# A fused clustered attention and two expert layers: cosines summed in one bank, and where second-layer products stand in a stage's last unit

## The chip, the cores and the metric

One core of a Trainium2 chip runs the whole program. The metric is the device time of one execution in microseconds (us). Engines are named as in the profile: PE is TensorE, PEld its weight loads, DVE is VectorE, ACT is ScalarE, POOL is GpSimd, and SP issues most transfers.

## What is computed

Attention over 2 batches, 8 heads, 768 positions of 64 numbers, in which a query sees only the keys that fall into its own cluster (the nearest of 16 centroids by cosine); then a layer with a softplus, and then eight experts whose results are weighted by a Sinkhorn-balanced gate.

```python
q_assign = argmax(einsum('bhsd,hcd->bhsc', q_n, c_n), axis=-1)     # k_assign likewise
mask = q_assign[:, :, :, None] == k_assign[:, :, None, :]
scores = where(mask, q @ k.T / sqrt(D), -1e9);  attn = softmax(scores) @ v
x = attn.transpose(0, 2, 1, 3).reshape(1536, 512)
x = (softplus(x @ w_in)) @ w_out                                   # 512 -> 2048 -> 512
out = sum_e P[:, e:e+1] * (relu(x @ w1[e]) @ w2[e])                # 512 -> 1024 -> 512, e < 8
```

## The kernel before

Numbers that need full precision are split into a high and a low part (names ending in h and l, or hi and lo), and products are made of the parts.

**Attention** works on eight pairs of heads, g = 0 to 7. `sched_pair` gives every preparation step of a pair a place on a common scale, the attention steps of the pair before it have theirs, and all are issued in that order; a scheduler then places the instructions of each engine. For a pair, `pair_sims` multiplies queries and keys with the centroids: `Z` (and `Z0` for the first pair) holds each centroid's high part in one set of columns and its low part in another, so that one half of a pair (`hf`) takes four products `sm` of 384 columns, and 128 rows come out: high and low sums apart. ACT copies them to `sT`, PE turns them over (`tp`, three per half), ACT copies the low half to `s2`, and DVE adds the two into `A` (L457). `pair_argmax` and `pair_ohT` make one-hot rows of it, which are sent into the operand `Bt` of the scores. Meanwhile four half-heads a pair run: scores `s` (L561), their maximum on DVE (L569), the exponential on ACT (L574), transposes `t` of it (L601), their split into `eh` (ACT, L604) and `el` (DVE, L608), the products `av` (L616), and a copy `tmp` (ACT, L628) when a half's products are complete. `tp`, `sm`, `t` and others share three banks of PSUM.

**The layers** are four stages: the softplus layer for batch 0 and 1, eight units each, then the experts for batch 0 and 1, 32 units each. A unit multiplies x with one block of weights, in seven products `group` (i = 0 to 6; banks la, lb and mb) or, in the first stage, four products `plain_group` (L767), and then applies the activation (`act`, `act_split`: `gf`, then `gh` on ACT L803 and `gl` on DVE L804). A second layer of four parts (`layer2`, L823 and L842) belongs to each unit; it runs one unit later, its parts standing between the next unit's products. In the last unit of a stage (`final`) no part stands between them: four parts of the unit before and then the four of the last unit itself follow its products. During that unit `x_split` also makes the next stage's operands (`chA`, `clA`, `chS`, `clS`, L97 and L99).

Of the kernel before, what the change touches and what calls it, by code (L numbers as in the profile page):

```python
# [7 lines left out]
F32 = mybir.dt.float32  # L8
F32R = mybir.dt.float32r
# [3 lines left out]
ALU = mybir.AluOpType  # L13
# [7 lines left out]
def attention_moe_moe2(ctx, tc, q, k, v, qt, kt, centroids, w_in, w_out, w_gate, w1, w2, eye, out, dbg=None):  # L21
    nc = tc.nc
    B, H, S, D = q.shape
    NC_ = centroids.shape[1]
# [16 lines left out]
    idf = const.tile([P, P], F32, tag="idf", name="idf")  # L41
# [47 lines left out]
    def x_split(key, blk, i):  # L89
        name = FIRST[i] if key == "1_0" else COMBOS[i]  # L90
        shape, mq = [P, KC // 2, S // 2], slot_pool["mq"]
        hi = mq.tile(shape, F32R, tag=f"ch{i}", name=f"ch{name}{key}", bufs=1)
        lo = mq.tile(shape, F32R, tag=f"cl{i}", name=f"cl{name}{key}", bufs=1)
        if key == "1_0":
            copy_r(hi, blk[name])
        else:
            (nc.vector.tensor_copy if i == 0 else nc.scalar.copy)(hi, blk[name])  # L97
        eng = nc.gpsimd if key == "1_0" or i in (1, 4, 5) else nc.vector
        eng.tensor_tensor(lo, blk[name], hi.bitcast(F32), ALU.subtract)  # L99
        XC[name] = hi, lo  # L100
# [141 lines left out]
    pp = prep.enter_context(tc.tile_pool(name="pp", bufs=1, side="right"))  # L242
# [4 lines left out]
    ps_m = ps_t  # L247
# [37 lines left out]
    def prep_z(c2):  # L287
        for i in range(2):
            pc = ps_m.tile([P, P], F32R, tag="t", name=f"pc{i}")
            nc.tensor.transpose(pc, c2[:, i].rearrange("p a d -> p (a d)"), idr)  # L290
            pv = pc.bitcast(F32).rearrange("p (h j c) -> p h j c", j=2, c=NC_)
            nc.vector.tensor_copy(Z0[:, :, 96 + 16 * i : 112 + 16 * i], pv[:, 0])
            for j in range(2):
                js, o = slice(j * D, (j + 1) * D), 64 + 32 * j + 16 * i
                nc.vector.tensor_copy(Z[js, :, o : o + NC_], pv[js, :, j])

# [15 lines left out]
    def at(step, fn, cat=None):  # L314
        events.append((step, len(events), fn, cat))
# [112 lines left out]
    def pair_sims(st, hf, ph):  # L428
        g = st.g
        if ph == 0:  # L430
            if hf == 0:
                st.sT = pp.tile([P, 2, CB], F32, tag="sT", name=f"sT{g}", bufs=1)
                st.A = pp.tile([P, 2, HT * 4, NC_], F32, tag="A", name=f"A{g}", bufs=1)
            st.sm = ps_m.tile([P, CB], F32, tag="t", name=f"sm{g}{hf}")
            for n in range(4):
                w, x = divmod(n, 2)
                if g:
                    c, m = Z[:, st.hp, 64 - 64 * w : 192 - 64 * w], st.HL[w][:, x]
                else:
                    o = 64 * w + 32 * x  # L440
                    c, m = Z0[:, x, 96 - o : 224 - o], st.AT[w, x]
                nc.tensor.matmul(st.sm, c, m[:, hf * CB : (hf + 1) * CB], start=n == 0, stop=n == 3)
        else:
            nc.scalar.copy(st.sT[:, hf], st.sm)

    def pair_simsT(st, hf, ph):
        g = st.g
        if ph == 0:
            st.tp = ps_m.tile([P, HT * 4, 2, NC_], F32, tag="t", name=f"tp{g}{hf}")
            tpv = st.tp.rearrange("p (t x) a c -> p t (x a c)", t=HT)  # L450
            for t in range(HT):
                nc.tensor.transpose(tpv[:, t, :], st.sT[:, hf, t * P : (t + 1) * P], idf)
        elif ph == 1:
            st.s2 = pp.tile([P, HT * 4, NC_], F32, tag="s2", name=f"s2{g}{hf}", bufs=1)
            nc.scalar.copy(st.s2, st.tp[:, :, 1, :])
        else:
            nc.vector.tensor_tensor(st.A[:, hf], st.tp[:, :, 0, :], st.s2, ALU.add)  # L457
# [47 lines left out]
    def sched_pair(g, b0):  # L505
        def P_(step, cat, fn, *args):
            def f():
                fn(pairs[g], *args)

            prep_fns.add(f)  # L510
            at(step, f, (cat, g))

        b0 += (2.06, -2.82)[g] if g < 2 else 0.0
        at(b0 - 12.13, lambda: pair_load(g))
        for n in range(4) if g == 0 else ():
            P_(b0 - 7.54 + 1.5 * n, "sp", pair_split, n)
        for w in range(2) if g else ():
            for ph in range(2):
                P_(b0 - 7 + 0.5 * ph + 3 * w, f"sp{ph}", pair_split_t, w, ph)
            P_(g * SP - 31 + 2 * w, "sp2", pair_split_t, w, 2)  # L520
        for n in range(2):
            P_(b0 + n + 1.54, "sq", pair_norm, n)
            P_(b0 + 4.27 + 2 * n, "red", pair_norm, 2 + n)
        P_(b0 + 8.02, "ln", pair_norm, 4)
        P_(b0 + 8.36, "nw", pair_norm, 5)
        P_(b0 + (12.5 if g else 8.37), "nv", pair_norm, 6)
        for i in range(8) if g == 0 else ():
            d = 1.09 * i
            P_(b0 + d + 0.5, "t0", pair_trans, i, 0)
            P_(b0 + d + 0.72, "t1", pair_trans, i, 1)  # L530
            P_(b0 + d + 1.9, "t2", pair_trans, i, 2)
        for hf in range(2):
            P_(b0 + hf + 8.27, "sm", pair_sims, hf, 0)
            P_(b0 + hf + 8.27 + .1, "smc", pair_sims, hf, 1)
            P_(b0 + 2 * hf + 11.5, "tp", pair_simsT, hf, 0)
            P_(b0 + 2 * hf + 11.5 + .1, "tpc", pair_simsT, hf, 1)
            P_(b0 + 2 * hf + 11.5 + 0.65, "tpa", pair_simsT, hf, 2)
            P_(b0 + hf + 22.92, "oh", pair_ohT, hf, 0)
            P_(b0 + hf + 22.92 + .1, "ohc", pair_ohT, hf, 1)
        for ph, stp in enumerate((14.5, 17.14, 17.6, 19.78, 21.61)):  # L540
# [102 lines left out]
    for i in range(NHALF):  # L643
        g = i // 4
        for t in range(HT):
            n = 6 * i + 2 * t - LEAD
# [6 lines left out]
        for s in range(NT):  # L653
            n = 6 * i + s
# [7 lines left out]
        at(92 + (n - 1) * 1.36, lambda n=n: fetch_first(n), ("fu", 0))  # L662
    for n in range(4):
        at(175 + n * 5, lambda n=n: x_split("1_0", first_blk, n), ("xs", 0))
    KEEP = {'sp2': 1, 'fr': 0, 'sq': 1, 'red': 1, 'av': 1, 'am3': 1, 'tpa': 1, 'smc': 0, 'm0': 1, 'nw': 0, 'nv': 1, 'rw': 1, 'pz': 1, 'e1': 1, 'ln': 0}
    events.sort(key=lambda x: x[:2])
    last_prep = max(key for key, _, fn, _ in events if fn in prep_fns)
    open_mq = True
    for key, _, fn, cat in events:
# [206 lines left out]
    sm = mp.tile([P, 2], F32, tag="gm", name="gm", bufs=1)  # L876
# [60 lines left out]
    def run(*steps):  # L937
        for l in steps:
            for fn in l:
                fn()  # L940

    run(*split_unit(units[0]))
    pend = []
    starts = [n for n in range(len(units)) if n == 0 or units[n - 1][:2] != units[n][:2]]
    for n, u in enumerate(units):
# [4 lines left out]
        hold = 0 <= held < NHOLD  # L950
# [23 lines left out]
        for i in range(7):  # L974
            if not is_plain(u):
                group(u, i)
            elif i % 2 == 0:
                plain_group(u, i // 2)
            run(steps.get(i, []))
            if n + 1 in starts:  # L980
                key = f"{units[n + 1][0]}_{units[n + 1][1]}"
                if not is_plain(u):
                    x_split(key, sums, i)
                else:
                    for c in ((4,), (5,), (0, 1), (), (), (), (2, 3, 6))[i]:
# [66 lines left out]
```

## Time and profile before

| | us |
|---|---|
| runs of the program, median of 3 | 1617.62 (1617.32 to 1620.14) |
| the profiled execution | 1615.32 |
| its span, first to last instruction | 1613.5 |
| PE busy | 1536.4 |
| DVE busy | 1079.2 |
| ACT busy | 851.7 |

The profiled execution is 2.3 us shorter than the median of the runs. A busy share is a mean over attention (to about 290 us) and four stages, each with a limit of its own, so the stretches have to be read apart.

### The profile page before, as it was taken

The page shows a single profiled execution, that of the slowest core. Times are in us where ns is not written, and L with a number is a line of the kernel's source. Part 1 is how long each engine was busy: PE and PEld are TensorE (multiplying, and loading weights), DVE is VectorE, ACT ScalarE, POOL GpSimd, SP SyncE. Part 2 cuts the span into 40 slices and gives each one's busy share as a digit, 9 for nine tenths or more (in the row PEclk, how much of TensorE's full clock was granted, in tenths as well). Part 3 has the DMA queues.
Part 4 walks back from the last instruction along what each step waited for, and adds up shares of the span by engine and source line. Part 5 has one row for each costly group of instructions (what it writes and reads, how often), then busy time and mean ns, then how long its engine had stood idle before and what let it go on. Part 6 is the DMA issues. An engine that isn't in the chain of part 4 may idle for free.

```text
span 1613.5 us, 22747 instructions
## 1 busy us (share of the span) xinstructions
PE 1536.4 (95%) x8134; PEld 1381.5 (86%) x8134; DVE 1079.2 (67%) x1772; ACT 851.7 (53%) x1727; POOL 687.2 (43%) x681
## 2 busy tenths in 40 slices
PE   5899999888999989999999999999999999999999
PEld 4788888787897868899999999988999999999997
DVE  5999999998554768665655656577655556565553
ACT  5888988766676754343434434344434434344342
POOL 4444533334755743434434443345333343343430
PEclk8999999999999999999999999999999999999999
DMA  7666620364211221222323223223223232232211
GB/s 218 179 168 167 177 65 7 124 219 143 78 58 53 59 60 54 84 60 83 75 66 89 62 79 74 77 66 115 64 77 86 58 86 65 76 78 73 79 53 46
DMA packets 135971, 145.18 MB, mean 90 GB/s; under 512 B 9169, under 2 KB 100785, under 8 KB 135857
## 3 DMA queue, kind: packets, MB, share of 16 engines
q1 hardware_dynamic: 135712, 143.66, 31.4%
q8 instruction: 64, 1.05, 0.3%
q14 instruction: 51, 0.41, 0.1%
q10 hardware_dynamic: 144, 0.07, 0.0%
HBM read 113.23 MB, written 11.58 MB: 77 GB/s over the span
## 4 chain that ended last, share of the span: by engine, by line
PE 64%; DVE 7%; ACT 4%; issue 1%; POOL 1%; DMA 0%; DVEq 0%; ACTq 0%; POOLq 0%
PE Y L842 32%; PE la L714 16%; PE mb L714 8%; PE lb L714 4%; PE y L823 2%; DVE gf L790 1%; DVE gl L804 1%; DVE wl L226 1%; ACT gh L803 1%; ACT u L788 1%; ACT u L787 1%; PE p L767 1%; ACT u L789 1%; DVE xS L75 0%; ACT wh L225 0%
## 5 line engine op out<-in xcount | busy, mean ns | idle before, releaser
L803 ACT CAST gh<-gf 128x384 fp32r<-128x384 f32 x316 | 161.5, 513 | 479.2 <-DVE gf L797 434.5
L214 POOL TENSOR_TENSOR wf<-wf 128x256 f32<-128x256 f32 x288 | 237.3, 846 | 346.9 <-DMA wf<-in_moe_w_dram 273.7
L232 POOL TENSOR_TENSOR w2l<-w2f,w2h 128x512 fp32r<-128x512 f32 x160 | 240.3, 1522 | 314.4 <-ACT w2h L231 314.4
L842 PE MATMUL Y<-w2h,gh 128*128 128x512 f32 x768 | 299.0, 389 | 0.7 <-ACT gh L803 0.7
L842 PE MATMUL Y<-w2l,gh 128*128 128x512 f32 x768 | 298.8, 389 | 0.0
L842 PE MATMUL Y<-w2h,gl 128*128 128x512 f32 x768 | 298.5, 389 | 0.0
L804 DVE TENSOR_TENSOR gl<-gf,gh 128x384 fp32r<-128x384 f32 x316 | 207.2, 659 | 96.1 <-ACT gh L803 89.4
L741 DVE TENSOR_TENSOR gf<-la,c 128x384 f32<-128x384 f32 x71 | 39.5, 557 | 254.2 <-PE la L714 254.0
L225 ACT CAST wh<-wf 128x512 fp32r<-128x512 f32 (+1 forms) x232 | 153.0, 684 | 35.1 <-PE la L714 24.8
L842 PEld LDWEIGHTS Y<-w2h,gl 128*128 128x128 f32 x768 | 144.1, 188 | 30.1
L842 PEld LDWEIGHTS Y<-w2h,gh 128*128 128x128 f32 x768 | 144.0, 188 | 22.3 <-ACT gh L803 1.2
L842 PEld LDWEIGHTS Y<-w2l,gh 128*128 128x128 f32 x768 | 144.2, 188 | 21.0
L797 DVE SCALAR_TENSOR_TENSOR gf<-gf,pb 128x384 f32<-128x384 f32 x177 | 151.1, 854 | 4.0
L226 DVE TENSOR_TENSOR wl<-wf,wh 128x512 fp32r<-128x512 f32 (+1 forms) x194 | 151.9, 809 | 1.0 <-ACT wh L225 0.9
L608 DVE TENSOR_TENSOR el<-t,eh 128x384 fp32r<-128x384 f32 x192 | 101.5, 544 | 11.8 <-ACT eh L604 10.6
L601 PE MATMUL t<-idf,E 128*128 128x128 f32 x576 | 96.4, 276 | 8.3 <-DVE el L608 5.0
L714 PE MATMUL mb<-chS,wh 128*128 128x384 f32 x288 | 98.2, 341 | 4.3 <-DVE gf L737 4.0
L604 ACT CAST eh<-t 128x384 fp32r<-128x384 f32 x192 | 91.6, 481 | 19.3 <-PE t L601 11.6
L231 ACT CAST w2h<-w2f 128x512 fp32r<-128x512 f32 x160 | 92.3, 618 | 16.7 <-PE y L823 8.7
L714 PE MATMUL la<-chA,wh 128*128 128x384 f32 x288 | 97.8, 340 | 1.6 <-DVE gf L797 1.6
L569 DVE TENSOR_REDUCE sc<-s 128x1 f32<-128x768 f32 x96 | 91.1, 949 | 12.0 <-PE s L561 11.4
L733 ACT COPY c<-la 128x384 f32<-128x384 f32 x144 | 68.8, 478 | 57.2 <-PE la L714 55.9
(210 smaller groups left out, 3478.0 us busy)
## 6 DMA issues: line engine op xcount, KB each, us to landing
w2f<-in_moe_w_dram SPq DMA_DIRECT2D x128, 256.0 KB, 3.4
wf<-in_moe_w_dram SPq DMA_DIRECT2D x128, 256.0 KB, 3.4
AT<-HL SPq DMA_DIRECT2D x56, 192.0 KB, 4.0
r<-in_moe_w_in_dram SPq DMA_DIRECT2D x16, 512.0 KB, 5.8
r<-in_moe_w_out_dram SPq DMA_DIRECT2D x16, 512.0 KB, 5.2
pb<-pdram SPq DMA_DIRECT2D x15, 384.0 KB, 7.6
Bt<-HL SPq DMA_DIRECT2D x28, 192.0 KB, 4.1
w<-wf SPq DMA_DIRECT2D x16, 256.0 KB, 3.5
```

Of the source, the lines that this page charges most:

```text
L214: nc.gpsimd.tensor_tensor(wf[:, SLOT[o_], :], wf[:, SLOT[u_], :], wf[:, SLOT[v_], :], ALU.subtract)
L225: nc.scalar.copy(wh[:, c0:c1], wf[:, c0 + o : c1 + o, :])
L226: (nc.vector if kind == 2 or u == (1, 0, 0, 0) else nc.gpsimd).tensor_tensor(wl[:, c0:c1], wf[:, c0 + o : c1 + o, :], wh[:, c0:c1].bitcast ...
L231: nc.scalar.copy(w2h[:, c], w2f[c])
L232: nc.gpsimd.tensor_tensor(w2l[:, c], w2f[c], w2h[:, c].bitcast(F32), ALU.subtract)
L601: nc.tensor.transpose(pt[:, t * P : (t + 1) * P], Et[i, t][:, s * P : (s + 1) * P], idf)
L608: nc.vector.tensor_tensor(el, TT.pop((i, s)), EHL[i, s].bitcast(F32), ALU.subtract)
L714: nc.tensor.matmul(ps, wt[:, s_, ks], xx[:, k_, :], start=i in (0, 1, 3) and n == 0, stop=n == 3 * nk - 1, skip_group_check=True,)
L797: nc.vector.scalar_tensor_tensor(g, src, 0.0, PB[sb, e][:, cols], ALU.max, ALU.mult)
L803: nc.scalar.copy(gh[:, cols], g)
L804: nc.vector.tensor_tensor(gl[:, cols], g, gh[:, cols].bitcast(F32), ALU.subtract)
L842: nc.tensor.matmul(y[m], gt[:, ms], wt[:, q, :], start=first and i == 0, stop=last and i == 2)
```

## The change

The low parts of the centroids move into an operand of their own, and eight products per half instead of four add high and low parts into one bank of 64 rows. `tp` has 64 columns, ACT copies it straight to `A`, and `s2` and the addition on DVE are gone; the entry `tpa`, which had kept that addition behind what was issued before it, is gone too. In the last unit of a stage the first two parts of the second layer are issued after products 1 and 3 as in other units, and two parts are left for the end.

```diff
-    Z = pp.tile([P, NPAIR, 192], F32R, tag="Z", name="Z", bufs=1)
+    Z = pp.tile([P, NPAIR, 2, 96], F32R, tag="Z", name="Z", bufs=1)
...
-            st.sm = ps_m.tile([P, CB], F32, tag="t", name=f"sm{g}{hf}")
-            for n in range(4):
-                w, x = divmod(n, 2)
+            st.sm = ps_m.tile([64, CB], F32, tag="t", name=f"sm{g}{hf}")
+            for n in range(8):
+                w, x, i = n // 4, n // 2 % 2, n % 2
...
-                nc.tensor.transpose(tpv[:, t, :], st.sT[:, hf, t * P : (t + 1) * P], idf)
-        elif ph == 1:
-            st.s2 = pp.tile([P, HT * 4, NC_], F32, tag="s2", name=f"s2{g}{hf}", bufs=1)
-            nc.scalar.copy(st.s2, st.tp[:, :, 1, :])
-        else:
-            nc.vector.tensor_tensor(st.A[:, hf], st.tp[:, :, 0, :], st.s2, ALU.add)
+                nc.tensor.transpose(tpv[:, t, :], st.sT[:, hf, t * P : (t + 1) * P], idf[:64, :64])
+        else:
+            nc.scalar.copy(st.A[:, hf], st.tp)
...
-            P_(b0 + 2 * hf + 11.5 + 0.65, "tpa", pair_simsT, hf, 2)
...
-            if (i % 2 == 1 or i == 6) and pend and not hold and not final:
+            if (i % 2 == 1 or i == 6) and pend and not hold and (i < 4 or not final):
                 layer2(pend[0], i // 2)
...
             if final:
-                for part in range(4):
+                for part in range(2, 4):
                     layer2(p_, part)
```

Where instructions move, at three places.

ACT in the start-up, where the first pair's cosines are copied (`sT`, `s` or `A`) while the second pair's operands `HL` and squares of `rawq` and `rawk` are made. Before:

```order
L395 ACTIVATE s_165<-s_165 128x24
L444 COPY sT_226<-sm_228 128x384
L360 ACTIVATE HL_256<-rT_202 128x768
L444 COPY sT_226<-sm_240 128x384
L455 COPY s_254<-tp_250 128x192
L360 ACTIVATE HL_272<-rT_204 128x768
L455 COPY s_268<-tp_264 128x192
L383 ACTIVATE rawq_206<-rawq_206 128x768
L383 ACTIVATE rawk_208<-rawk_208 128x768
```

and in the changed kernel:

```order
L395 ACTIVATE s_165<-s_165 128x24
L360 ACTIVATE HL_263<-rT_202 128x768
L444 COPY sT_226<-sm_228 64x384
L360 ACTIVATE HL_276<-rT_204 128x768
L383 ACTIVATE rawq_206<-rawq_206 128x768
L444 COPY sT_226<-sm_244 64x384
L454 COPY A_227<-tp_258 128x192
L383 ACTIVATE rawk_208<-rawk_208 128x768
L454 COPY A_227<-tp_270 128x192
```

The second `sT` copy now stands behind both `HL` and the square of `rawq`, and the last copy, to `A`, behind `rawk` as well.

DVE in the last unit of the first stage (unit 7; `gf` and `gl` are its activation, `chA` and `clA` the next stage's operands). Before:

```order
L804 TENSOR_TENSOR gl_0_6_5277<-gf_0_6_5275,gh_0_6_5276 128x384
L97 CAST chA_1_5460<-x_70 128x768
L99 TENSOR_TENSOR clA_1_5461<-x_70,chA_1_5460 128x768
L790 SCALAR_TENSOR_TENSOR gf_0_7_5413<-p_0_7_5400,u_0_7_00_5416 128x384
L804 TENSOR_TENSOR gl_0_7_5415<-gf_0_7_5413,gh_0_7_5414 128x384
L790 SCALAR_TENSOR_TENSOR gf_0_7_5448<-p_0_7_5435,u_0_7_10_5451 128x384
L804 TENSOR_TENSOR gl_0_7_5450<-gf_0_7_5448,gh_0_7_5449 128x384
```

and in the changed kernel:

```order
L800 TENSOR_TENSOR gl_0_6_5309<-gf_0_6_5307,gh_0_6_5308 128x384
L786 SCALAR_TENSOR_TENSOR gf_0_7_5445<-p_0_7_5432,u_0_7_00_5448 128x384
L800 TENSOR_TENSOR gl_0_7_5447<-gf_0_7_5445,gh_0_7_5446 128x384
L97 CAST chA_1_5504<-x_70 128x768
L99 TENSOR_TENSOR clA_1_5505<-x_70,chA_1_5504 128x768
L786 SCALAR_TENSOR_TENSOR gf_0_7_5492<-p_0_7_5479,u_0_7_10_5495 128x384
L800 TENSOR_TENSOR gl_0_7_5494<-gf_0_7_5492,gh_0_7_5493 128x384
```

The first activation of unit 7, `gf` and `gl` (L786 and L800 are L790 and L804 of before), has moved ahead of `chA` and `clA`.

PE in the last unit of the third stage, from the end of its second product (bank lb) on; `Y` is the second layer. Before:

```order
L714 MATMUL lb_7_3_11285<-clA_0_6797,wh_7_3_11129 128x384
L714 MATMUL lb_7_3_11285<-chA_0_6796,wl_7_3_11131 128x384
L714 MATMUL la_7_3_11266<-chS_0_6810,wh_7_3_11129 128x384
L714 MATMUL la_7_3_11266<-clS_0_6811,wh_7_3_11129 128x384
L714 MATMUL la_7_3_11266<-chS_0_6810,wl_7_3_11131 128x384
L714 MATMUL la_7_3_11266<-chS_0_6810,wh_7_3_11129 128x384
L714 MATMUL la_7_3_11266<-clS_0_6811,wh_7_3_11129 128x384
L714 MATMUL la_7_3_11266<-chS_0_6810,wl_7_3_11131 128x384
L842 MATMUL Y_0_7623<-w2h_7_2_10989,gh_7_2_11144 128x512
L714 MATMUL mb_7_3_11318<-chS_0_6825,wh_7_3_11129 128x384
L714 MATMUL mb_7_3_11318<-clS_0_6826,wh_7_3_11129 128x384
```

and in the changed kernel:

```order
L710 MATMUL lb_7_3_11317<-clA_0_6829,wh_7_3_11161 128x384
L710 MATMUL lb_7_3_11317<-chA_0_6828,wl_7_3_11163 128x384
L838 MATMUL Y_0_7655<-w2h_7_2_11021,gh_7_2_11176 128x512
L838 MATMUL Y_0_7655<-w2l_7_2_11023,gh_7_2_11176 128x512
L838 MATMUL Y_0_7655<-w2h_7_2_11021,gl_7_2_11177 128x512
L838 MATMUL Y_1_7656<-w2h_7_2_11021,gh_7_2_11176 128x512
L838 MATMUL Y_1_7656<-w2l_7_2_11023,gh_7_2_11176 128x512
L838 MATMUL Y_1_7656<-w2h_7_2_11021,gl_7_2_11177 128x512
L838 MATMUL Y_2_7657<-w2h_7_2_11021,gh_7_2_11176 128x512
L838 MATMUL Y_2_7657<-w2l_7_2_11023,gh_7_2_11176 128x512
L838 MATMUL Y_2_7657<-w2h_7_2_11021,gl_7_2_11177 128x512
L710 MATMUL la_7_3_11298<-chS_0_6854,wh_7_3_11161 128x384
```

Nine products of the second layer, one part, now stand behind lb, and none behind the third product; the next part stands behind mb.

## Rows read from the trace of the kernel before

**Rows 1.** The page: span, and busy time of each engine.

```profile
span 1613.5 us, 22747 instructions
...
PE 1536.4 (95%) x8134; PEld 1381.5 (86%) x8134; DVE 1079.2 (67%) x1772; ACT 851.7 (53%) x1727; POOL 687.2 (43%) x681
```

**Rows 2.** Windows: us, then PE, PEld, DVE, ACT, POOL busy (instructions), PEclk, DMA, GB/s.

```profile
160.28:191.82 31.54, 29.68 (x196) 26.95 (x195) 29.56 (x60) 28.49 (x65) 15.59 (x21) 1.00 0.64 181
254.00:285.00 31.00, 28.99 (x192) 26.33 (x191) 28.24 (x53) 26.02 (x59) 5.28 (x6) 1.00 0.00 1
```

**Rows 3.** Timeline of TensorE: start, us, line, what.

```profile
162.36 0.87 PE L442 MATMUL sm<-HL,Z 128*128 128x384 f32 x4
163.06 0.49 PE L601 MATMUL t<-idf,E 128*128 128x128 f32 x3
163.31 0.60 PE L561 MATMUL s<-AT,AT 128*128 128x384 f32 x2
```

**Rows 4.** Timeline of ScalarE, the copy that closes each half's product.

```profile
162.83 0.48 ACT L628 COPY tmp<-av 64x384 f32<-64x384 f32 x1
...
171.02 0.47 ACT L628 COPY tmp<-av 64x384 f32<-64x384 f32 x1
...
178.27 0.48 ACT L628 COPY tmp<-av 64x384 f32<-64x384 f32 x1
...
187.07 0.47 ACT L628 COPY tmp<-av 64x384 f32<-64x384 f32 x1
...
263.80 0.47 ACT L628 COPY tmp<-av 64x384 f32<-64x384 f32 x1
...
270.85 0.48 ACT L628 COPY tmp<-av 64x384 f32<-64x384 f32 x1
```

**Rows 5.** Timeline of VectorE, last of one arg-max's four steps.

```profile
178.16 0.55 DVE L480 TENSOR_TENSOR OH<-A,mx 128x384 fp32r<-128x384 f32 x1
```

**Rows 6.** Groups by line, 0 to 300 us: busy, mean ns, idle before.

```profile
L457 DVE TENSOR_TENSOR A<-tp,s 128x192 f32<-128x192 f32 x16 | 5.6, 348 | 1.9 <-ACT s L455 1.9
...
L455 ACT COPY s<-tp 128x192 f32<-128x192 f32 x16 | 5.2, 327 | 0.8 <-ACT E L574 0.4 <-PE tp L452 0.2
```

**Rows 7.** Timeline of all engines, start-up.

```profile
12.14 2.30 PE L442 MATMUL sm<-AT,Z 128*128 128x384 f32 x8
...
14.89 0.47 ACT L444 COPY sT<-sm 128x384 f32<-128x384 f32 x1
...
16.40 0.87 ACT L383 ACTIVATE rawq<-rawq 128x768 f32<-128x768 f32 x1
...
16.95 1.27 DVE L469 TENSOR_TENSOR A<-A,nrm 128x384 f32<-128x384 f32 x1
...
24.55 2.85 PE L442 MATMUL sm<-HL,Z 128*128 128x384 f32 x8
...
25.34 2.47 SPq L501 DMA_DIRECT2D Bt<-OHT  x4
...
28.29 0.95 PE L561 MATMUL s<-Bt,Bt 80*128 80x384 f32 x4 [0.89 <-DMA Bt<-OHT]
```

**Rows 8.** Windows of TensorE: us, PE busy (instructions), PEclk, DMA, GB/s.

```profile
31.00:37.00 6.00, 6.00 (x22) 0.50 0.97 236
```

**Rows 9.** Timeline of TensorE, last units of three stages: idle time before it.

```profile
426.68 0.44 PE L767 MATMUL p<-chA,wh 128*128 128x384 f32 x1 [1.83 <-DVE gf L790]
...
565.40 0.44 PE L714 MATMUL mb<-chS,wh 128*128 128x384 f32 x1 [1.59 <-DVE gf L737]
...
584.15 0.62 PE L823 MATMUL y<-gl,w2h 128*128 128x512 f32 x2 [1.99 <-DVE gl L804]
...
1089.58 0.45 PE L714 MATMUL mb<-chS,wh 128*128 128x384 f32 x1 [1.77 <-DVE gf L737]
```

**Rows 10.** Timeline of VectorE at the end of the third stage.

```profile
1098.59 3.71 DVE L804 TENSOR_TENSOR gl<-gf,gh 128x384 fp32r<-128x384 f32 x3
```

**Rows 11.** The chain that ended last, end of the program.

```profile
1593.37 16.33 PE Y L842 x72
```

More of the change, by code (lines that the diff above doesn't have):

```diff
@@ L251, in attention_moe_moe2 @@
         nc.gpsimd.memset(wsel[:, :, c : c + 1], float(NC_ - c))
-    Z = pp.tile([P, NPAIR, 192], F32R, tag="Z", name="Z", bufs=1)
-    Z0 = pp.tile([P, 2, 224], F32R, tag="Z0", name="Z0", bufs=1)
+    Z = pp.tile([P, NPAIR, 2, 96], F32R, tag="Z", name="Z", bufs=1)
+    Z0 = pp.tile([P, 2, 2, 112], F32R, tag="Z0", name="Z0", bufs=1)
     def norm_newton(o, x, s0, eng):
@@ L291, in prep_z @@
             pv = pc.bitcast(F32).rearrange("p (h j c) -> p h j c", j=2, c=NC_)
-            nc.vector.tensor_copy(Z0[:, :, 96 + 16 * i : 112 + 16 * i], pv[:, 0])
+            nc.vector.tensor_copy(Z0[:, :, i, 48:64], pv[:, 0])
             for j in range(2):
-                js, o = slice(j * D, (j + 1) * D), 64 + 32 * j + 16 * i
-                nc.vector.tensor_copy(Z[js, :, o : o + NC_], pv[js, :, j])
+                js, o = slice(j * D, (j + 1) * D), 32 + NC_ * j
+                nc.vector.tensor_copy(Z[js, :, i, o : o + NC_], pv[js, :, j])
     def last_of_engines(engines):
@@ L431, in pair_sims @@
             if hf == 0:
-                st.sT = pp.tile([P, 2, CB], F32, tag="sT", name=f"sT{g}", bufs=1)
+                st.sT = pp.tile([64, 2, CB], F32, tag="sT", name=f"sT{g}", bufs=1)
                 st.A = pp.tile([P, 2, HT * 4, NC_], F32, tag="A", name=f"A{g}", bufs=1)
-            st.sm = ps_m.tile([P, CB], F32, tag="t", name=f"sm{g}{hf}")
-            for n in range(4):
-                w, x = divmod(n, 2)
+            st.sm = ps_m.tile([64, CB], F32, tag="t", name=f"sm{g}{hf}")
+            for n in range(8):
+                w, x, i = n // 4, n // 2 % 2, n % 2
                 if g:
-                    c, m = Z[:, st.hp, 64 - 64 * w : 192 - 64 * w], st.HL[w][:, x]
+                    c, m = Z[:, st.hp, i, 32 - 32 * w : 96 - 32 * w], st.HL[w][:, x]
                 else:
-                    o = 64 * w + 32 * x
-                    c, m = Z0[:, x, 96 - o : 224 - o], st.AT[w, x]
-                nc.tensor.matmul(st.sm, c, m[:, hf * CB : (hf + 1) * CB], start=n == 0, stop=n == 3)
+                    o = 32 * w + 16 * x
+                    c, m = Z0[:, x, i, 48 - o : 112 - o], st.AT[w, x]
+                nc.tensor.matmul(st.sm, c, m[:, hf * CB : (hf + 1) * CB], start=n == 0, stop=n == 7)
         else:
@@ L448, in pair_simsT @@
         if ph == 0:
[L449 to L450 removed]
+            st.tp = ps_m.tile([P, HT * 4, NC_], F32, tag="t", name=f"tp{g}{hf}")
+            tpv = st.tp.rearrange("p (t x) c -> p t (x c)", t=HT)
             for t in range(HT):
[L452 to L455 removed]
+                nc.tensor.transpose(tpv[:, t, :], st.sT[:, hf, t * P : (t + 1) * P], idf[:64, :64])
         else:
[L457 removed]
+            nc.scalar.copy(st.A[:, hf], st.tp)
     def pair_argmax(st, ph):
@@ L664, in attention_moe_moe2 @@
         at(175 + n * 5, lambda n=n: x_split("1_0", first_blk, n), ("xs", 0))
-    KEEP = {'sp2': 1, 'fr': 0, 'sq': 1, 'red': 1, 'av': 1, 'am3': 1, 'tpa': 1, 'smc': 0, 'm0': 1, 'nw': 0, 'nv': 1, 'rw': 1, 'pz': 1, 'e1': 1, 'ln': 0}
+    KEEP = {'sp2': 1, 'fr': 0, 'sq': 1, 'red': 1, 'av': 1, 'am3': 1, 'smc': 0, 'm0': 1, 'nw': 0, 'nv': 1, 'rw': 1, 'pz': 1, 'e1': 1, 'ln': 0}
     events.sort(key=lambda x: x[:2])
```

## The prediction, made before the changed kernel ran

> **What bounds the kernel now.** I read the page first: PE is busy 1536.4 of 1613.5 us [rows 1], so on the whole TensorE sets the time. That mean hides where it waits. The timeline of PE with its idle times shows no wait at all in the last stage, and only a few in the others; those in the last units of the first three stages are [rows 9]. Attention, to about 290 us, is the other place that the change touches, and there the page cannot say who sets the pace: over one pair (31.5 us) PE is busy for 29.7 us and DVE for 29.6 us [rows 2].
>
> The copies that close each half-head settle it [rows 4]. Without any preparation beside it a half takes 270.85 - 263.80 = 7.05 us. The half from 171.02 to 178.27 holds a whole arg-max on DVE, four steps of about 0.55 us each [rows 5], and takes 7.25 us: 2.2 us more for DVE cost 0.2 us. The half from 162.83 to 171.02 has little more for DVE, but a group of `sm` and both groups of `tp` on PE, and takes 8.19 us. The half behind 178.27, in which PE turns over the one-hot rows and waits for them, takes 8.80 us. So more PE work makes a half longer, and more DVE work hardly does. In attention PE sets the pace, with about 1.9 us of idle time in a pair [rows 2].
>
> **The added products.** Four `sm` run from 162.36 to 163.06 [rows 3]: 0.175 us each. The change has eight more for a pair: 1.40 us. Six of the eight pairs are prepared beside running halves, which makes 8.4 us of PE work. That is the upper bound; the lower is what is left if the 1.9 us of idle time per pair took in most of it. I don't see PE idle near the `sm` in the timeline, but a part of its waits for `el` later in the pair should shrink, because DVE loses two additions of 0.348 us [rows 6] and each half lasts longer. The six transposes of a pair also have 64 columns instead of 128; three of the present shape take 163.31 - 163.06 = 0.25 us [rows 3], so half of two such groups, 0.25 us a pair, is the most that can go, and I take half of that. I take 1.40 - 0.13 - 0.4 = 0.85 us a pair, **+5.0 us for six pairs**, with +1.5 (0.25 us a pair) and +8.4 (nothing given back) as bounds.
>
> A product with a stationary operand half as wide fills half of the array, and one could hope that it costs half. The trace of before has no `sm` of 64 columns. The Trainium skill (TensorE: Matmul & The Clock Gate, "Wait — 56ns, not 53.3ns?") speaks against that hope and so against this change: the distance from one product to the next is the number of moving columns over the clock plus about 2.5 ns, with nothing of the stationary width in it. By that rule 384 columns are an estimated 162 ns and the six pairs cost 7.8 us where my rows give 8.4 us.
>
> **The removed additions.** Sixteen on DVE, 0.348 us each, 5.6 us [rows 6], of which twelve lie in the running part (4.2 us). Since a half hardly notices DVE work, I book nothing beyond the 0.4 us a pair above. If DVE were the limit after all, they would give 4.2 us. The copy on ACT stays; it only writes `A` in place of `s2`.
>
> **The start-up** is a chain: cosines of pair 0, copies, arg-max, one-hot rows, the transfer to `Bt`, first complete score. Two things make it later. First the copies. Now eight `sm` run from 12.14 to 14.44 and the arg-max begins at 16.95 [rows 7]. After the change the first `sT` copy can start when eight are done, about 14.5. Behind it stand, by the order, `HL`, `rawq`, the second `sT`, a copy to `A`, `rawk` and the last copy: 0.47 + 0.87 + 0.87 + 0.47 + 0.33 + 0.87 + 0.33 = 4.2 us with the durations of [rows 6, 7] (`HL` and `rawk` taken as long as `rawq`). The arg-max then begins at 18.7: +1.8 us. Second, the `sm` of pair 1 stand on PE ahead of the first scores with `Bt`. Eight take 2.85 us there, and the scores now begin at 28.29, 0.89 us after them, when the transfer is in. Shifted by 1.8 us, sixteen begin at 26.35 and end between 30.5 (second half at the full clock) and 31.9 (all at the pace of 2.85 us for eight), while the transfer is in at 30.1. So the first scores start 2.2 to 3.6 us later; I take 2.6.
>
> Some of this can come back. From 31 to 37 us PE is busy without a break at a granted clock of 0.50, the 1.2 GHz level [rows 8]; before that, between 27.4 and 31 us, it had done little but the four scores at 28.29 [rows 7]. With twice the products PE is busier ahead of this stretch, and at the full clock its six us would be three. The Trainium skill (TensorE: Matmul & The Clock Gate, "Part 1: The HAM clock gate") says that the array starts at half its clock and that sustained activity releases it, which would make this gain likely; the trace agrees in that the low clock follows the idle stretches. I book a third of the 3 us: the start-up is **+1.6 us**, from -0.8 (2.2 - 3.0) to +3.6.
>
> **The last units of stages.** The second layer's instructions stay the same in number, so only waits can go.
>
> - First stage: product 3 waits 1.83 us for `gf`, which has to empty its bank and stands behind `chA` and `clA` on DVE [rows 9]. Now `gf` stands ahead of them, and two parts of some 2.1 us each lie between. The whole wait goes: -1.8 us. The end stays covered: two parts of the unit before, 4.2 us, and the first of the unit's own stand ahead of the one that needs the last product.
> - Second stage: the wait of 1.59 us at 565.40 is covered by a part. But the end of this stage waits for DVE: the last `gl` is awaited at 584.15 for 1.99 us [rows 9]. DVE and ACT have the same work as before ahead of that `gl`, with fewer products to cover it. I take -1.2 us; 0 and -2.0 are the bounds.
> - Third stage: the wait of 1.77 us at 1089.58 [rows 9] is covered in the same way. The three last `gl` ran from 1098.59 to 1102.3 [rows 10], just in time for the last unit's own parts, which followed without a wait; those would now come some 2 us earlier and wait for them. I take -1.2 us, from 0 to -2.0.
> - Fourth stage: the trace has no wait; the second layer runs as one block of 16.33 us, 72 products, to the end [rows 11]. Where 18 of them stand changes nothing: 0.
>
> Sum **-4.2 us**, from -1.8 to -5.8.
>
> **Sum**: +5.0 + 1.6 - 4.2 = +2.4 us. Against the profiled execution's own 1615.3 us that is 1617.7. The runs' median lies 2.3 us above that execution, so I forecast 1620.0 us. A measurement of this kernel can tell about 0.2% (3.2 us) from no change, and +2.4 is within that.
>
> **Rivals.**
>
> - *Slower: every added product is paid.* Place: PE's queue in the halves that prepare a pair. For it speaks that no idle time stands near the `sm`, against it that 1.9 us a pair stand elsewhere. Price 8.4 instead of 5.0: 1.6 + 8.4 - 4.2 = +5.8, 1623.4 us. It decides once a pair lasts over 32.9 us where [rows 2] have 31.5. Chance 0.20.
> - *Slower: the waits at the stage ends only move.* DVE in the second and third stage is late in any case, and the change doesn't do there what it says; only the first stage gains. 5.0 + 1.6 - 1.8 = +4.8, 1622.4 us. For it: the waits on `gl`; against: in the third stage there is none now. Chance 0.16.
> - *Faster: DVE sets the pace of attention.* For it: PE's waits there are mostly for `el`, and DVE is as busy as PE. Against: the half with the arg-max. Then -4.2 for the additions, the products hide in PE's idle time, and 1.6 - 4.2 - 4.2 = -6.8, 1610.8 us. Chance 0.18.
> - *The clock stays up in the start-up*: -0.8 in place of +1.6, sum 0, 1617.6 us. Chance 0.14.
>
> **How the numbers follow.** My forecast keeps 0.32; its own range, from half its terms' bounds, is 1616 to 1624 us. Of it 0.20 fall within 0.2%, 0.08 above and 0.04 below. The first rival is slower (0.20), the second mostly (0.10 of 0.16), the third faster (0.18), the fourth the same, with 0.04 faster. That makes faster 0.26, same 0.36, slower 0.38. The terms' bounds together reach from -5.1 (all low) to +10.2 us; leaving out half of the faster rival and the sum of all high bounds gives 1612 to 1626 us.
>
> **What the changed profile would show.** Halves with `sm` longer by about 0.5 us, a pair at 32.4 us, and DVE's busy share in attention lower. The first score with `Bt` at 30.5 to 31 us instead of 28.29. No wait of PE for `gf` in the last units of the first three stages, but 1 to 2 us of waiting for `gl` behind them in the second and third. I am wrong if a pair gets shorter, if the clock in the start-up changes much, or if the scheduler's other order in attention, which moves many scores and transposes by a place or two, costs or gives more than the counted work.

## The result, and the profile after

The changed kernel takes 1630.83 us (median of 4 runs, 1629.65 to 1632.31), the kernel before 1618.82 us beside it. The ratio is 1.0079, with a 95% interval of 1.0067 to 1.0091: 12 to 13 us slower, above the range of 1612 to 1626 us. In what follows, us on the kernel before are ratio minus 1, times 1618.

The page of the changed kernel, span and engines; its counterpart is [rows 1]:

```profile
span 1630.5 us, 22858 instructions
...
PE 1555.6 (95%) x8198; PEld 1389.1 (85%) x8198; DVE 1081.1 (66%) x1756; ACT 853.6 (52%) x1727; POOL 687.3 (42%) x681
```

PE has 64 products more, and 19 us more of busy time. The windows over one pair, from the first `sm` of one to the first `sm` of the next, with columns as in [rows 2]:

```profile
168.72:202.95 34.23, 31.68 (x204) 27.46 (x202) 29.00 (x56) 28.85 (x65) 15.25 (x21) 1.00 0.51 134
```

A pair took 31.54 us and takes 34.23. PE is busy 2.0 us longer, DVE 0.6 us less, and PE's idle time did not shrink: 1.86 us before, 2.55 now. The timeline of PE in that pair says what the products cost:

```profile
168.72 1.54 PE L442 MATMUL sm<-HL,Z 128*64 128x384 f32 x8
170.09 0.51 PE L557 MATMUL s<-AT,AT 128*128 128x384 f32 x2
...
177.61 0.40 PE L452 MATMUL tp<-idf,sT 64*128 64x64 f32 x3
177.94 0.61 PE L557 MATMUL s<-AT,AT 128*128 128x384 f32 x2
```

Eight products with a stationary operand of 64 columns last 1.37 us up to the next instruction, 0.171 us each; the four of 128 columns took 0.70 us [rows 3]. So the width of that operand gives nothing back. The Trainium skill (TensorE: Matmul & The Clock Gate, "Wait — 56ns, not 53.3ns?") has only the moving columns in its rule, and the trace agrees: 0.171 us with 64 stationary columns, 0.175 with 128. The three narrow transposes `tp` take 0.33 us up to what follows, three wide ones in the same pair of the kernel before 0.32:

```profile
165.13 0.49 PE L452 MATMUL tp<-idf,sT 128*128 128x128 f32 x3
165.45 0.49 PE L601 MATMUL t<-idf,E 128*128 128x128 f32 x3
```

The copies that close a half on ACT:

```profile
189.39 0.48 ACT L624 COPY tmp<-av 64x384 f32<-64x384 f32 x1
...
198.19 0.47 ACT L624 COPY tmp<-av 64x384 f32<-64x384 f32 x1
...
206.06 0.48 ACT L624 COPY tmp<-av 64x384 f32<-64x384 f32 x1
...
215.52 0.47 ACT L624 COPY tmp<-av 64x384 f32<-64x384 f32 x1
...
223.65 0.48 ACT L624 COPY tmp<-av 64x384 f32<-64x384 f32 x1
```

The half with the one-hot rows still takes 8.80 us, as in [rows 4]; the one with the second group of `sm` and `tp` takes 9.46 us, where a like half took 8.19.

At one place in attention PE waits longer than the kernel before does anywhere behind its first score with `Bt` (there 1.71 us at most). It is where PE turns over the one-hot rows `OH` of the third pair, whose last step runs on POOL. The timeline of PE at this place, before and then after:

```profile
82.00 0.50 PE L490 MATMUL po<-idr,OH 128*64 128x128 f32 x3 [1.07 <-DVE el L608]
```

```profile
85.72 0.38 PE L487 MATMUL po<-idr,OH 128*64 128x128 f32 x3 [2.36 <-POOL OH L480]
```

The place lies in the second four halves. Cut at the copies `tmp`, these four are, before and then after:

```profile
81.42:113.69 32.27, 29.96 (x188) 26.83 (x189) 30.02 (x61) 28.67 (x64) 16.64 (x20) 0.95 0.62 158
83.84:119.73 35.89, 31.98 (x200) 28.72 (x201) 33.09 (x63) 29.59 (x66) 17.39 (x22) 0.95 0.63 166
```

PE's idle time in them grew from 2.31 to 3.91 us. The mean granted clock (PEclk) is 0.95 in both: it falls here in either kernel, so the fall is no part of the difference.

Start-up, all engines (counterparts in [rows 7]):

```profile
12.06 4.55 PE L442 MATMUL sm<-AT,Z 128*64 128x384 f32 x16
...
16.74 0.46 ACT L444 COPY sT<-sm 64x384 f32<-64x384 f32 x1
...
18.05 0.30 ACT L454 COPY A<-tp 128x192 f32<-128x192 f32 x1
...
18.39 1.23 DVE L466 TENSOR_TENSOR A<-A,nrm 128x384 f32<-128x384 f32 x1 [3.46 <-ACT A L454]
...
24.52 5.08 PE L442 MATMUL sm<-HL,Z 128*64 128x384 f32 x16
...
29.43 0.87 PE L557 MATMUL s<-Bt,Bt 80*128 80x384 f32 x4
```

The arg-max begins 1.4 us later, behind the last copy to `A`, which waits its turn on ACT. The first score with `Bt` follows right behind the sixteen products of the second pair, which run to 29.6 us, and is only 1.1 us later than before. Last, the end of the third stage on PE (counterpart: 1089.58 in [rows 9]) and on DVE (counterpart: [rows 10]):

```profile
1104.11 0.45 PE L710 MATMUL mb<-chS,wh 128*128 128x384 f32 x1 [0.84 <-DVE gf L733]
...
1110.37 0.44 PE L710 MATMUL la<-chA,wh 128*128 128x384 f32 x1 [0.75 <-DVE gf L737]
...
1118.27 0.50 PE L838 MATMUL Y<-w2h,gl 128*128 128x512 f32 x1 [2.01 <-DVE gl L800]
```

```profile
1114.04 2.62 DVE L99 TENSOR_TENSOR clA<-x,chA 128x768 fp32r<-128x768 f32 x1
1116.58 3.19 DVE L800 TENSOR_TENSOR gl<-gf,gh 128x384 fp32r<-128x384 f32 x2
```

One wait of 1.77 us has become three, of 3.6 us together. The last stage still ends with one block of the second layer, now of 54 products instead of 72 [rows 11], 17.0 us later:

```profile
1614.47 12.25 PE Y L838 x54
```

Between the two profiled executions, attention (up to the first `p` of the layers: 289.73 and 305.33) accounts for 15.6 of these 17.0 us. The profiled execution of before is 3.5 us under the median of its runs, that of after 1.5 us above, so 5.0 us of the 17.0 come from the choice of executions.

### The profile page after: what moved, and what is told of

It is laid out like the page before. It is cut to its first block, busy times and chain, and to the rows that moved or that the text cites. A ratio compares the mean times of both kernels' runs of the same rounds, so it can differ in the third digit from the quotient of the medians.

```text
span 1630.5 us, 22858 instructions
## 1 busy us (share of the span) xinstructions
PE 1555.6 (95%) x8198; PEld 1389.1 (85%) x8198; DVE 1081.1 (66%) x1756; ACT 853.6 (52%) x1727; POOL 687.3 (42%) x681
## 4 chain that ended last, share of the span: by engine, by line
PE 63%; DVE 8%; ACT 4%; issue 1%; DMA 1%; POOL 0%; DVEq 0%; ACTq 0%; SPq 0%; POOLq 0%
PE Y L838 31%; PE la L710 16%; PE mb L710 8%; PE lb L710 4%; PE y L819 3%; DVE gf L786 1%; DVE gl L800 1%; PE p L763 1%; DVE wl L226 1%; ACT gh L799 1%; ACT u L784 1%; DVE gf L793 1%; ACT u L783 1%; DVE xS L75 1%; ACT u L785 1%
## 5 line engine op out<-in xcount | busy, mean ns | idle before, releaser
L800 DVE TENSOR_TENSOR gl<-gf,gh 128x384 fp32r<-128x384 f32 x316 | 207.4, 659 | 96.3 <-ACT gh L799 89.7
L793 DVE SCALAR_TENSOR_TENSOR gf<-gf,pb 128x384 f32<-128x384 f32 x177 | 155.4, 878 | 4.0
L604 DVE TENSOR_TENSOR el<-t,eh 128x384 fp32r<-128x384 f32 x192 | 101.4, 545 | 12.8 <-ACT eh L600 12.2
L231 ACT CAST w2h<-w2f 128x512 fp32r<-128x512 f32 x160 | 92.3, 617 | 11.8 <-PE y L819 5.5
L710 PE MATMUL la<-chS,wh 128*128 128x384 f32 x288 | 97.8, 340 | 0.4 <-ACT c L729 0.4
```

Source lines behind the costliest of these rows:

```text
L231: nc.scalar.copy(w2h[:, c], w2f[c])
L604: nc.vector.tensor_tensor(el, TT.pop((i, s)), EHL[i, s].bitcast(F32), ALU.subtract)
L710: nc.tensor.matmul(ps, wt[:, s_, ks], xx[:, k_, :], start=i in (0, 1, 3) and n == 0, stop=n == 3 * nk - 1, skip_group_check=True,)
L793: nc.vector.scalar_tensor_tensor(g, src, 0.0, PB[sb, e][:, cols], ALU.max, ALU.mult)
L800: nc.vector.tensor_tensor(gl[:, cols], g, gh[:, cols].bitcast(F32), ALU.subtract)
```

## The experiments

The first four runs were made against three theories. **A:** TensorE pays for each added product, and the new order of its queue costs something on top. **B:** the loss comes from the order that the scheduler makes without the entry `tpa`, and added products hide in idle time. **C:** much of the loss lies in the stage ends.

**e1_cosines.** The change with the stage ends put back:

```diff
-            if (i % 2 == 1 or i == 6) and pend and not hold and (i < 4 or not final):
+            if (i % 2 == 1 or i == 6) and pend and not hold and not final:
...
-                for part in range(2, 4):
+                for part in range(4):
```

> Only the cosines are changed, the last units of stages are as before. Theory A (TensorE pays each added product, and the new order of the queue on top): nearly the whole loss of the change is here, +10 to +13 us on the kernel before. Theory C (the stage ends, where the third stage grew by about 3 us, carry much of the loss): +6 us or less. The prediction's own terms say +6.6.

Ratio 1.0084 (1.0069 to 1.0100): +13.6 us. The cosines carry the whole loss; C falls.

**e2_stage_ends.** The same lines the other way round, on the kernel before.

> Only the last units of stages are changed, the cosines are as before. Theory A: the gain of the second stage (about 2.6 us between the two profiles) and the loss at the end of the third (about 3 us) cancel, -1.5 to +1.5 us. Theory C: +4 us or more. The prediction's own term says -4.2.

Ratio 0.9989 (0.9978 to 1.0000): -1.8 us. It goes the way of the prediction's term (-4.2), at less than half its size. The two halves add up: 13.6 - 1.8 = 11.8, and the change measured 12 to 13.

**e3_products_twice.**

```diff
-            for n in range(4):
-                w, x = divmod(n, 2)
+            for n in range(8):
+                w, x = divmod(n // 2, 2)
...
-                nc.tensor.matmul(st.sm, c, m[:, hf * CB : (hf + 1) * CB], start=n == 0, stop=n == 3)
+                nc.tensor.matmul(st.sm, c, m[:, hf * CB : (hf + 1) * CB], start=n == 0, stop=n == 7)
```

> The kernel before with each of the four products of a half made twice into the same bank (cosines come out doubled, which no maximum notices); 128 rows, the copy of the low half, the addition on DVE and its pin stay. Theory A: counted work alone, 8.4 us for six pairs and 1 to 2 us in the start-up, +8 to +11 us, a pair at 33 us or more. Theory B (the new order of the queue, for want of the pin, makes the loss, and added products hide in idle time): +1.5 to +5 us.

Ratio 1.0066 (1.0051 to 1.0080): +10.7 us. B falls. Two pairs of this run in windows:

```profile
166.88:199.73 32.85, 31.04 (x203) 28.30 (x203) 28.75 (x58) 28.65 (x65) 15.22 (x21) 1.00 0.53 139
199.73:233.61 33.88, 31.44 (x203) 28.32 (x203) 28.88 (x58) 28.73 (x65) 15.24 (x21) 1.00 0.40 100
```

PE is busy 31.0 and 31.4 us, 1.4 and 1.8 more than in [rows 2], and idle for 1.8 and 2.4 us: in these two pairs no idle time took anything in. The wait at the one-hot rows is here too:

```profile
83.38 0.37 PE L490 MATMUL po<-idr,OH 128*64 128x128 f32 x3 [2.36 <-POOL OH L483]
```

**e5_unpinned.** `'tpa': 1` is taken out of the kernel before.

> The kernel before with nothing changed but the entry tpa, which is taken out, so that the addition is no longer held behind what was issued before it. Theory A: within 2 us of before. Theory B: +5 us or more, with the waits of TensorE for el and for the one-hot rows that the changed kernel shows.

Ratio 1.0009 (0.9999 to 1.0019): +1.5 us, not told from zero. A alone is left, but e1 costs 3 us more than e3 (their intervals overlap).

**e6_no_low.** e1 with four products:

```diff
-            for n in range(8):
-                w, x, i = n // 4, n // 2 % 2, n % 2
+            for n in range(4):
+                w, x, i = n // 2, n % 2, 0
```

> The changed cosines (stage ends as before) with four products of 64 rows in place of eight: the low parts of the centroids are left out. Theory A (the counted products make the loss): 1618 to 1621 us, that is no more than e5_unpinned, 11 us or more under e1_cosines. Theory B (the new order, the lost pin and the copy behind the transposes make it): 1625 us or more. If the narrower transposes and the missing additions were worth something, it would come out below the kernel before.

Ratio 1.0037 (1.0022 to 1.0052): +6.0 us, between the theories. It is 7.6 us under e1, so the products are the larger part; but without them the new cosines still lose 6 us, against A's figure. The trace shows where: its halves from the second four to the fifth are as long as before (table below), but the first `tmp` comes at 49.68 us instead of 46.10, and the first four halves behind it take 1.7 us longer. The first score with `Bt` waits 3.40 us for its transfer and starts 1.85 us later than in [rows 7], and the granted clock stays at 0.50, the 1.2 GHz level, up to 43 us, where [rows 8] have it until 37:

```profile
30.14 1.62 PE L557 MATMUL s<-Bt,Bt 80*128 80x384 f32 x4 [3.40 <-DMA Bt<-OHT]
```

```profile
34.00:37.00 3.00, 3.00 (x12) 2.29 (x11) 2.01 (x3) 2.25 (x9) 0.68 (x3) 0.50 0.99 255
37.00:40.00 3.00, 3.00 (x14) 2.61 (x13) 0.84 (x3) 1.76 (x5) 0.84 (x1) 0.50 1.01 228
40.00:43.00 3.00, 3.00 (x14) 2.81 (x13) 2.01 (x4) 1.85 (x4) 0.00 (x0) 0.50 0.16 56
```

**e8_two_pairs_twice.** The edit of e3 with `k = 1 if g > 1 else 2` products of a kind.

> The kernel before with the products of the first two pairs alone made twice, so that only the start-up gets longer. By the prediction's start-up term +1.6 us (bounds -0.8 to +3.6); by e3_products_twice less 8.4 us, +2.2.

Ratio 0.9996 (0.9987 to 1.0005): -0.6 us. Sixteen products in place of eight in the start-up cost nothing that the runs can tell. In its trace the clock is at 1.00 from 28 us on and the first `tmp` comes at 44.69 us, 1.4 us earlier than in the trace of before and 0.3 earlier than in e2's (44.98), which has the same attention as before.

**e9_twice_unpinned.** e3 without the entry `tpa`.

> e3_products_twice without the entry tpa. If the products and the lost pin simply add up, +12 us on the kernel before, and e1_cosines (+13.6 by its medians) is explained but for 1 to 2 us. If the pin matters more where TensorE has more to do, +14 or more; if the layout of 64 rows costs something by itself, +11 or less.

Ratio 1.0060 (1.0048 to 1.0072): +9.7 us, not more than e3. The pin is no part of the loss.

What makes e1 cost 3 to 4 us more than twice the products was then put to three theories: **D**, the missing addition and its pin; **E**, the layout of 64 rows; **F**, the order that the scheduler happens to make.

**e10_no_addition.** e3 without `tpa`, and

```diff
-            nc.scalar.copy(st.s2, st.tp[:, :, 1, :])
-        else:
-            nc.vector.tensor_tensor(st.A[:, hf], st.tp[:, :, 0, :], st.s2, ALU.add)
+            nc.scalar.copy(st.A[:, hf], st.tp[:, :, 0, :])
```

> 128 rows and each product made twice as in e3_products_twice, but the copy of the low half, the addition and its pin are gone: ACT copies the high half straight to A, and the low parts of the cosines are left out. Open is why the changed cosines cost 3 to 4 us more than twice the products do. Theory D (the missing addition and its pin change what waits for what): +13 us on before, as e1_cosines. Theory E (the layout of 64 rows: its narrow transposes and the restarts around them): +10 us or less.

Ratio 1.0055 (1.0042 to 1.0067): +8.9 us. D falls. Sixteen additions less on DVE bring 0.8 us beside e9 and 1.8 beside e3, with intervals that overlap.

**e11_addition_kept.** e1 with `tpa` put back, and

```diff
-            nc.scalar.copy(st.A[:, hf], st.tp)
+            nc.scalar.copy(st.s2, st.tp)
+        else:
+            nc.vector.tensor_tensor(st.A[:, hf], st.tp, st.s2, ALU.add)
```

> The changed cosines, 64 rows and eight products, with a copy to s2 on ACT, an addition on DVE (of the cosines to themselves, which doubles them) and the entry tpa put back. Theory D: +10 us on before. Theory E: +13 us or more.

Ratio 1.0073 (1.0060 to 1.0085): +11.8 us, between D and E; it decides nothing by itself.

**e12_copy_later.** e1, and

```diff
-            P_(b0 + 2 * hf + 11.5 + .1, "tpc", pair_simsT, hf, 1)
+            P_(b0 + 2 * hf + 11.5 + .65, "tpc", pair_simsT, hf, 1)
```

with `'tpc': 1` put into `KEEP`.

> e1_cosines with the copy to A listed half a step later and held behind what was issued before it, so that the scheduler makes another order of the same instructions. Theory F (the order that the scheduler happens to find decides those 3 to 4 us): at least 2 us away from e1_cosines. Theories D and E: within 2 us of it, +12 to +15 us on before.

Ratio 1.0061 (1.0049 to 1.0073): +9.9 us, 3.7 under e1 with the very same instructions. That is what F forecast, though the two intervals just overlap; the change itself, whose cosines are those of e1, stands with e1 (12.8 us, and 14.6 without the -1.8 of e2). E falls as well: in this order 64 rows without the addition cost no more than the 128 rows of e9 (+9.7). The same two windows of the start-up, first of e1, then of e12:

```profile
34.00:37.00 3.00, 3.00 (x13) 2.00 (x13) 1.80 (x4) 2.42 (x7) 0.68 (x3) 0.50 0.94 234
37.00:40.00 3.00, 3.00 (x14) 2.83 (x14) 1.78 (x3) 1.78 (x4) 0.84 (x1) 0.58 0.91 219
```

```profile
34.00:37.00 3.00, 3.00 (x20) 2.51 (x21) 2.19 (x5) 3.00 (x9) 0.78 (x3) 1.00 0.85 221
37.00:40.00 3.00, 3.00 (x23) 2.87 (x23) 3.00 (x7) 2.80 (x7) 0.68 (x2) 1.00 0.93 202
```

In six us in which PE is busy throughout, e12 gets 43 instructions done and e1 27, and the first `tmp` comes at 43.88 instead of 47.18 us. Ahead of these windows both traces have the same wait of PE, 1.73 us, over at 32.18 us in e1 and at 31.24 in e12. The table has the start of the first `tmp` and then the length of each following four halves; the first six of these hold the preparation of a pair, the last none. One trace each, in us:

| | first tmp | 1 | 2 | 3 | 4 | 5 | 6 | 7 |
|---|---|---|---|---|---|---|---|---|
| before | 46.10 | 35.32 | 32.27 | 32.32 | 32.26 | 31.96 | 32.05 | 28.57 |
| changed | 47.05 | 36.79 | 35.89 | 33.99 | 35.67 | 34.26 | 33.93 | 28.86 |
| e1_cosines | 47.18 | 36.84 | 35.93 | 33.95 | 34.27 | 34.28 | 33.98 | 28.87 |
| e12_copy_later | 43.88 | 35.26 | 35.92 | 33.48 | 34.99 | 34.25 | 33.83 | 28.59 |
| e3_products_twice | 46.58 | 34.91 | 37.20 | 34.60 | 32.88 | 33.83 | 33.49 | 28.61 |
| e9_twice_unpinned | 43.54 | 35.15 | 37.05 | 34.60 | 32.91 | 32.87 | 33.39 | 28.57 |
| e6_no_low | 49.68 | 36.98 | 32.05 | 32.56 | 32.45 | 31.76 | 33.35 | 28.38 |

How far such lengths repeat, four traces tell that hold the attention code of the kernel before (before, e2, e7, e13). Their first `tmp` lies between 44.98 and 46.44 us, and the clock in the start-up is not the same in them; from 34 to 37 us, in before and in e2:

```profile
34.00:37.00 3.00, 3.00 (x14) 2.90 (x13) 1.44 (x3) 2.50 (x7) 0.57 (x3) 0.50 0.92 236
34.00:37.00 3.00, 3.00 (x22) 2.79 (x20) 2.52 (x5) 2.92 (x9) 0.68 (x3) 0.93 0.96 234
```

Behind it their columns agree within 0.1 us, except where the clock falls differently, which makes up to 1.5 us. Such a fall stands in column 4 of the changed kernel and of e12 and in column 6 of e6. The changed kernel's column 4, and that of e1, which has the same cosines:

```profile
153.72:189.39 35.67, 33.10 (x204) 28.93 (x203) 29.06 (x56) 28.96 (x64) 15.24 (x21) 0.95 0.56 153
153.90:188.17 34.27, 31.72 (x204) 27.48 (x203) 29.01 (x56) 28.89 (x65) 15.27 (x21) 1.00 0.57 159
```

The start and the first column are 83.84 us together in the changed kernel and 79.14 in e12, so in these traces most of what the order costs lies there. How much of that is the order and how much the single execution stays open: e3 and e9 are 2.8 us apart in the same place (81.49 and 78.69), and 1.0 us in their runs.

What the products cost stands in columns 1 to 6. Together they grow by 10.7 us in e3 and 9.8 in e9, where 8.4 were counted, but not evenly: column 2, with the wait at the one-hot rows, by 4.9 and 4.8, the other five by 5.8 and 5.0, which is 1.2 and 1.0 each and under the 1.40 of a pair's products. Columns 2 and 4 of e3, and column 4 of before:

```profile
81.49:118.69 37.20, 32.28 (x200) 29.28 (x201) 32.85 (x64) 30.01 (x67) 17.29 (x22) 0.95 0.61 161
153.29:186.17 32.88, 31.04 (x204) 28.30 (x203) 29.10 (x59) 28.65 (x64) 15.21 (x21) 1.00 0.58 159
```

```profile
146.01:178.27 32.26, 29.68 (x196) 27.02 (x195) 30.78 (x62) 29.06 (x65) 16.22 (x21) 1.00 0.60 161
```

In column 2 PE's idle time grows from 2.31 us before to 4.92, in column 4 it shrinks from 2.58 to 1.84. In e1 it does not shrink there (2.55), and its five other columns grow by 1.9 each.

**e7_two_stages.** The kernel before, with parts of the second layer between the products in the last units of the first two stages alone:

```diff
-            if (i % 2 == 1 or i == 6) and pend and not hold and not final:
+            if (i % 2 == 1 or i == 6) and pend and not hold and (not final or i < 4 and n + 1 in starts[:3]):
...
-                for part in range(4):
+                for part in range(2 if n + 1 in starts[:3] else 0, 4):
```

> The kernel before with parts of the second layer between the products in the last units of the first two stages alone; the third and fourth end as before. If the third stage's end gives back what the first two gain, as the traces with and without that edit say (it lost about 2 us from the first Y on), this is 3 to 4.5 us faster than before; if the trace of before was only a lucky one, -1.8 us as e2_stage_ends.

Ratio 0.9975 (0.9966 to 0.9985): -4.0 us. This beats both kernels. The 1.83 us of [rows 9] in the first stage are gone from its trace. In the last unit of the second stage, the kernel before has three more waits beside the 1.59 and 1.99 of [rows 9], which makes 5.3 us:

```profile
561.92 0.44 PE L714 MATMUL la<-chS,wh 128*128 128x384 f32 x1 [0.24 <-ACT c L733]
...
578.04 0.62 PE L823 MATMUL y<-gh,w2h 128*128 128x512 f32 x2 [0.31 <-ACT gh L803]
...
579.90 0.50 PE L823 MATMUL y<-gl,w2h 128*128 128x512 f32 x1 [1.13 <-DVE gl L804]
```

In e7 they are others, and 3.5 us together:

```profile
563.95 0.45 PE L714 MATMUL mb<-chS,wh 128*128 128x384 f32 x1 [0.59 <-DVE gf L737]
...
569.71 0.44 PE L714 MATMUL la<-chA,wh 128*128 128x384 f32 x1 [0.23 <-DVE gf L741]
...
576.46 0.39 PE L823 MATMUL y<-gl,w2h 128*128 128x256 f32 x1 [1.09 <-DVE gl L804]
...
579.13 0.96 PE L823 MATMUL y<-gh,w2h 128*128 128x512 f32 x3 [1.22 <-ACT gh L803]
...
582.78 0.62 PE L823 MATMUL y<-gl,w2h 128*128 128x512 f32 x2 [0.41 <-DVE gl L804]
```

**e13_third_stage.** The same edit with `starts[3:]`.

> The kernel before with parts of the second layer between the products in the last unit of the third stage alone. If that stage's end gives back what the first two gain (e2_stage_ends -1.8 us, e7_two_stages -4.0 us), this is slower than before, by 1.5 to 3 us, with a wait for the last gl that before does not have. By the prediction's term for this stage it is 1.2 us faster (0 to 2.0).

Ratio 1.0014 (1.0006 to 1.0023): +2.3 us, and with -4.0 this makes the -1.8 of e2. Its timeline of PE:

```profile
1097.73 0.45 PE L714 MATMUL la<-chA,wh 128*128 128x384 f32 x1 [0.67 <-DVE gf L741]
...
1105.61 0.50 PE L842 MATMUL Y<-w2h,gl 128*128 128x512 f32 x1 [2.02 <-DVE gl L804]
```

## Why the prediction was wrong

**The added products** (+5.0, bounds +1.5 to +8.4) are the step that failed; with the start-up they made +6.6 for the cosines, which measured +13.6 (e1). The price of one product was right: 0.175 us forecast, 0.171 measured. Three things were wrong in what I made of it.

- I took all six pairs to be alike, at 0.85 us, and had no price for the one-hot rows. PE waits 2.36 to 2.38 us for those of the third pair in all seven kernels with the products of every pair doubled (the change, e1, e3, e9 to e12), and 1.08 us at most at this place in the others. Column 2 grew by 3.6 to 4.9 us in each such kernel of the table, and not in e6. That the doubled products make those rows late follows from this comparison; which instruction of the chain is late was not tested by itself.
- The 0.4 us a pair for shrinking waits came in e3 and e9, outside column 2, and not in the order of the changed kernel: e1's other columns grew by 1.9 us each. Why the idle time shrinks in one order and not in the other was not tested.
- The 0.13 us for the narrower transposes don't exist: three of them take 0.33 us up to what follows, and 0.32 with 128 columns.

So the first rival, every added product paid, came nearest: its point (a pair over 32.9 us) is passed by the 34.23 us, and its 8.4 us are most of e3's 10.7 and e9's 9.7. But it had the sum, not the place: almost half of the growth in e3 and e9 is column 2. That the upper bound of 8.4 was too low has the same reason.

**The removed additions** are worth little (e10: 0.8 to 1.8 us, not told from zero, where that rival had 4.2 and all products hidden). PE sets the pace, and the rival in which DVE does falls. In reading [rows 4] and [rows 5] I was off by a little: the last of the four steps begins at 178.16, so about 1.7 us of the arg-max and not 2.2 lie in the half that ends at 178.27, and the `sm` at 162.36 stand mostly ahead of the half that I counted them to.

**The start-up** (+1.6). The copies held up the arg-max by 1.4 us where I had 1.8. I let the sixteen products of the second pair begin 1.8 us later for it; they began at 24.52 us, as before (24.55), and the first score with `Bt` came 1.1 us later, not 2.6. By e8 the added products cost -0.6 us there (-2.1 to +0.8), with the clock up sooner in its trace. In the changed kernel's trace it was not: first `tmp` +0.95, the four halves behind it +1.5. I had named the scheduler's order as a danger and gave it no price; e1 and e12 put it at 3.7 us, and the clock of the start-up is where the two traces differ most. Why the clock stays up in one and falls in the other is not settled, and four traces of one code differ in it too.

**The stage ends** (-4.2) measured -1.8. The first two stages, forecast at -3.0 together, gave -4.0 (e7; -5.5 to -2.4). The first stage's wait of 1.83 us went as forecast. In the second, the waits of the last unit went from 5.3 to 3.5 us (3.6 in the changed kernel, but 4.8 in e2, which has the same code there), where I had 1.2 less; three of the old ones I had overlooked, since [rows 9] lack them. So the second rival, in which those waits only move, is at most half right there. I don't place the 4.0 us more closely, since stretches of the layers differ by up to 2.7 us between traces of the same code (first stage: 156.65 us in before, 159.35 in e5). In the third I was wrong in sign: -1.2 forecast, +2.3 measured. I had seen that the last `gl` came just in time [rows 10], and counted on them to stay where they were. But the two parts now delay the products from which `gf` and so `gl` are made. In the changed kernel those `gl` ended 17.5 us later than before (1102.30 and 1119.77), the unit itself started 13.65 us later (1084.24 and 1097.89), and PE waited for them 2.01 us. This miss of 3.5 us is smaller than that of the cosines, 7.0.

## What to carry to other kernels

Where one engine sets the pace, idle time elsewhere in its queue is no sure credit for added work: here some of it shrank in one order and none in another. Book added instructions at their full duration until a trace shows otherwise, and look for the hand-over with the least slack, here the one-hot rows of one pair, which cost more than the products of any other. Work put between the products of a unit covers a wait for the result of an earlier one, and delays everything that is made from the later ones; it helps only where what comes after them has slack. And an edit that makes a scheduler find another order can have a price of its own, here some 4 us between two orders, which a run with the same instructions in a third order shows. Before a length of one trace is laid to such an order, traces of the same code tell how much it varies by itself.

## What the runs showed of the hardware

Transposes of 64 columns on 64 rows, three in a group, take no less than those of 128 (0.33 us; 0.32 us, and 0.25 in [rows 3]). A fall of the granted clock amid the halves cost about 1.4 us (35.67 and 34.27 us for the same work); in the kernel before it stood at 0.50 from 82 to 85 us, behind three waits of PE of 0.75, 0.82 and 1.07 us between 76 and 82 us.

In the start-up, the first finished half came between 43.54 and 49.68 us in kernels of nearly the same work: earliest, up to 44.69 us, in the three whose clock was at 1.00 from 28 us on (e8, e9, e12), latest in e6, whose clock was at 0.50 until 43 us. The Trainium skill (TensorE: Matmul & The Clock Gate, "Part 1: The HAM clock gate") says that the array starts throttled and activity releases it. The traces agree in that the low clock stands behind stretches in which PE was mostly idle: in before it was busy for 1.00 of the 3 us from 28 to 31, and [rows 8] follow. That rule alone doesn't tell e1 from e12, which have the same products, nor e6 from before, which have as many in the start-up.
